# A scheduled attention-and-MLP kernel: two cross-engine latencies in the builder's simulation are changed, and the engine lists are made anew

## The chip, the cores and the metric

The kernel runs on one core of one Trainium2 chip. TensorE (PE) multiplies matrices, with its weight loads listed apart as PEld; VectorE (DVE), ScalarE (ACT) and GpSimd (POOL) do the elementwise work, and SyncE (SP) issues most of the DMAs. Each engine takes its own list of instructions in order and waits on semaphores that the others raise. The metric is the device time of one execution in microseconds (us).

## The reference

`x` has 2048 rows of 512. Part A goes through the sequence in 64 segments of 32 rows, and each segment needs eight memory rows that the segment before it made. Part B is an MLP over all rows. Cut to what matters:

```
for s in range(64):
    h = concat([mem, xs_s])                      # 8 memory rows and 32 rows of the sequence
    q, k, v = h @ Wq, h @ Wk, h @ Wv             # 32 heads of 128
    p = softmax(where(mask, q @ k.T * scale, -1e9))
    o = (p @ v) @ Wo
    mem = o[:8]; outs.append(o[8:])              # mem goes into the next segment
h  = x + concat(outs)                            # A works on layernorm(x)
h2 = h + gelu(layernorm(layernorm(h)) @ w1 + b1) @ w2 + b2
```

## The kernel before

The builder doesn't emit instructions as it goes. It records operations (`Op`: engine, tensors read and written, an assumed duration) into a `Sched` object, which then decides the order on every engine. TensorE's order is written out by hand (`ORDERS` and `EDGE`, for the segments in the middle and in the first and last block). For the other engines `schedule` ranks the operations by the longest path behind them (with a table of bonuses), then places them one by one, by rank, into the earliest stretch of their engine that is free in a simulation. The simulated start of an operation is the latest end of what it depends on plus `lat(p, o)`, a latency that depended only on the engine of the producer (`HOP`). The engine lists, and with them the semaphore waits, follow from the simulated starts. On the chip nothing of the simulated times is left, only the order.

Four segments of 32 rows make a block of 128 rows; I call them positions 0, 1, 2 and 3 of the block. One segment takes about 10.5 us and has on each half `r` of the heads this chain, with line numbers of the profile:

- TensorE makes K, Q and V of the segment (L676, and L417 where the weights stay loaded). ScalarE copies K and Q out of PSUM (`kq`, L690 and L691), and VectorE transposes them into `KALL` and `QX` (L713).
- TensorE makes the memory rows' scores (L831). `sc_softmax` follows: VectorE takes the maximum `nmc` (L839), ScalarE the exponentials `EC` (L843), VectorE the reciprocal `rsc` of their sum (L846), the product `PC` (L849) and its transpose `PTC` (L850).
- TensorE multiplies `PTC` with V (L861, L865), and the heads' output with Wo (L960). VectorE transposes that (`TT`, L972) and adds its halves into `hT` (L966), the memory rows of the next segment, with which TensorE starts over.

Work that can wait goes in between. `wo_B` puts the memory-row outputs of one whole block through Wo; VectorE transposes them into `TTB` (L985, position 3) and adds them into `opT` (L988, two instructions, position 0 of the next block). `nat` then turns a finished block: SyncE issues a DMA transpose of `opT` to `oN` (L993), VectorE adds it to the rows `xr` (L996) and takes their statistics (L999, L1000), GpSimd makes a scale of them (L1001, L1002), and SyncE writes the rows out (L1003). `ln1` prepares a block three ahead: statistics (L616, L617), scale on GpSimd (L618, L619), normalized rows `xn` (L620), a DMA transpose to `xT` (L637) and two GpSimd copies into `hT` and `hB` (L640, L639). The same SyncE list holds the transfers that spread a block's memory-row values over partitions, out to `v_last` (L773) and back into `VBD` (L778). GpSimd's copy into `QX` (L732) also belongs to every segment.

The two lines that the change speaks of by name are kinds of operations: `EC0` and `EC1` are the exponentials of the two halves, `hTm` is the sum that makes the memory rows (L966).

Of the kernel before, what the change touches and what calls it, by code (L numbers as in the profile page):

```python
# [16 lines left out]
ENGINES = ("pe", "act", "dve", "pool", "sp")  # L17
HOP = {"pe": 0.21, "act": 0.06, "dve": 0.05, "pool": 0.08, "sp": 2.0}
SWITCH = 0.12
OVERLAP = {"act": 0.1, "dve": 0.07, "pool": 0.05, "sp": 0.0}  # L20
DMA_SEMS, SOFT_SEMS = 100, 8
FETCH_N, FETCH_US, FETCH_OFF = 254.4, 3.5, 90
# [66 lines left out]
class Sched:  # L89
# [81 lines left out]
    @staticmethod  # L171
    def lat(p, o):
        if p.is_dma:
            return HOP["sp"]
        if p.eng == "pe" and o.eng == "pe":
            return 0.0
        return HOP[p.eng]

    def schedule(self):
        assert len(self.pe_order) == len(set(self.pe_order)) == sum(o.eng == "pe" for o in self.rec)  # L180
# [45 lines left out]
        for o in order:  # L226
# [5 lines left out]
            if o.eng == "pe":  # L232
                if o.prev is not None:
                    q = o.prev
                    t = max(t, q.start + q.dur + (SWITCH if q.mode != o.mode else 0.0))
                fetched += o.ni
# [7 lines left out]
            for eng, (fn, dur) in (o.alts or {o.eng: (o.fn, o.dur)}).items():  # L244
                L, ST = lines[eng], starts[eng]
                u = t
                while True:
                    i = bisect.bisect_right(ST, u)
                    while True:
# [3 lines left out]
                        if prev is not None:  # L253
                            s = max(s, prev.start + prev.dur - OVERLAP[eng])
                        if nxt is None or s + dur - OVERLAP[eng] <= nxt.start + 1e-9:
                            break
# [1057 lines left out]
```

## Time and profile before

| what | value |
|---|---|
| median of 3 runs | 830.18 us (829.86 to 830.25) |
| the profiled execution | 829.23 us, of which its span is 827.5 us |
| granted TensorE clock, mean | 0.994 |
| instructions | 46217 |
| DVE busy | 541.4 us (65%) |
| ACT busy | 581.2 us (70%) |
| POOL busy | 80.6 us (10%) |

A span runs from the first to the last instruction of the program. In a timeline a row has the start in us from the span's start, the busy time, engine, line, operation and operands, the count of instructions merged into it, and in brackets the idle time of the engine before it with what ended that. In the chain of work that ended last, a row has a start, a length and the work.

### The profile page before, as it was taken

To read this page: it belongs to the slowest core of one execution; us is meant where nothing else is said; L and a number is where in the kernel's file an instruction comes from. 1 tells how busy PE (TensorE), PEld (TensorE's weight loads), DVE (VectorE), ACT (ScalarE), POOL (GpSimd) and SP (SyncE) were. 2 spreads that over 40 slices of the span, in tenths; PEclk is the share of its full clock that TensorE was granted. 3 is DMA by queue.
4 is the path that set the end of the run, shared out by engine and by line. 5 is a ranking of instruction groups with operands and counts; after the bars stand their busy time and mean duration, and the time that the engine had idled before them with its cause. 6 is when DMAs were issued, how large, how long until landed. Compare 5 with 4: busy or idle time off the path is not lost.

```text
span 827.5 us, 46217 instructions
## 1 busy us (share of the span) xinstructions
PE 791.1 (96%) x22113; PEld 384.4 (46%) x19913; DVE 541.4 (65%) x1716; ACT 581.2 (70%) x1570; POOL 80.6 (10%) x210
## 2 busy tenths in 40 slices
PE   4788999999999999999999999999999998899998
PEld 1244444444545454545454545454545454554443
DVE  3258677777777777777777777777777777533211
ACT  2457787878787878787878787878787877533332
POOL 4002100001010001010100000000000000015200
PEclk9899999999999999999999999999999999999999
DMA  9960100111101111111110101000000111353310
GB/s 344 386 189 17 23 23 23 30 30 29 30 27 27 31 27 30 30 30 29 30 30 29 31 25 33 20 20 24 23 23 23 48 31 30 99 155 88 71 32 26
DMA packets 62283, 46.37 MB, mean 56 GB/s; under 512 B 28336, under 2 KB 58424, under 8 KB 62088
## 3 DMA queue, kind: packets, MB, share of 16 engines
q1 hardware_dynamic: 61692, 42.94, 17.5%
q8 instruction: 165, 2.70, 1.4%
q0 software_dynamic: 208, 0.33, 0.1%
q14 instruction: 30, 0.25, 0.1%
q10 hardware_dynamic: 188, 0.14, 0.1%
HBM read 28.98 MB, written 8.39 MB: 45 GB/s over the span
## 4 chain that ended last, share of the span: by engine, by line
PE 84%; ACT 5%; SPq 5%; DVE 4%; DMA 1%; issue 1%
PE ps L676 20%; PE ps L960 19%; PE quad L676 11%; PE quad L417 9%; PE ps L1196 6%; PE quad L1203 6%; PE ps L417 4%; PE quad L861 3%; ACT kq L690 3%; PE ps L831 3%; SPq L587 2%; SPq L602 2%; PE ps L889 2%; PE quad L918 1%; DVE KALL L713 1%; DMA WO<-in_A_Wo_dram 1%
## 5 line engine op out<-in xcount | busy, mean ns | idle before, releaser
L960 PE MATMUL ps<-WO,OT 128*32 128x256 bf16 x4224 | 140.7, 274 | 4.4 <-ACT OT L690 2.8
L676 PE MATMUL ps<-WV,hT 128*32 128x512 bf16 x1640 | 122.2, 381 | 0.0
L417 PE MATMUL quad<-WK,hT 128*32 128x512 bf16 x1204 | 112.1, 379 | 0.0
L960 PEld LDWEIGHTS ps<-WO,OT 128*32 128x32 bf16 x4224 | 94.9, 96 | 34.8 <-ACT OT L690 19.4
L972 DVE STREAM_TRANSPOSE TT<-ps 128x256 f32<-128x256 f32 x66 | 29.7, 450 | 107.5 <-PE ps L960 107.5
L690 ACT CAST OT<-quad 128x128 bf16<-128x128 f32 (+1 forms) x192 | 84.9, 442 | 20.7 <-PE quad L865 11.9
L690 ACT CAST kq<-quad 128x512 bf16<-128x512 f32 x128 | 69.5, 588 | 26.9 <-PE quad L417 23.9
L843 ACT ACTIVATE EC<-ps,nmc 128x64 f32<-128x64 f32 x256 | 78.0, 310 | 12.8 <-DVE nmc L839 4.9
L713 DVE STREAM_TRANSPOSE KALL<-kq 128x256 f32<-128x256 f32 x160 | 71.1, 445 | 22.1 <-ACT kq L690 17.2
L676 PE MATMUL quad<-WK,hT 128*32 128x512 bf16 x844 | 84.2, 389 | 0.0
L1199 ACT ACTIVATE WQ<-ps,b1t 128x512 bf16<-128x512 f32 x56 | 38.5, 687 | 58.7 <-PE ps L1196 58.7
L690 ACT CAST VS<-ps 128x512 bf16<-128x512 f32 x128 | 75.0, 586 | 2.5 <-PE ps L417 2.5
L676 PE MATMUL quad<-WQ,hT 128*32 128x512 bf16 x856 | 60.6, 380 | 5.2 <-DVE hT L966 5.2
L691 ACT ACTIVATE kq<-ps 128x512 bf16<-128x512 f32 x96 | 57.6, 600 | 8.4 <-PE ps L676 6.0
L676 PEld LDWEIGHTS quad<-WK,hT 128*32 128x32 bf16 x844 | 25.9, 99 | 80.3 <-issue 78.3
L901 ACT ACTIVATE SA<-SA 128x256 f32<-128x256 f32 x64 | 26.7, 417 | 51.5 <-DVE SA L900 50.6
L713 DVE STREAM_TRANSPOSE QX<-kq 128x256 f32<-128x256 f32 x128 | 56.3, 440 | 3.8 <-ACT kq L691 3.8
L676 PE MATMUL ps<-WQ,hT 128*32 128x512 bf16 x772 | 56.2, 379 | 0.0
L1203 PE MATMUL quad<-WK,WQ 128*128 128x512 bf16 (+1 forms) x228 | 54.6, 376 | 0.5 <-DVE WV L1255 0.5
L691 ACT ACTIVATE kq<-quad 128x512 bf16<-128x512 f32 x64 | 38.1, 595 | 19.3 <-PE quad L417 16.0
L843 ACT ACTIVATION_READ_ACCUMULATOR EC<-ps,nmc 128x1 f32 x256 | 50.4, 197 | 0.0
L1255 DVE TENSOR_TENSOR WV<-quad,WV 128x512 bf16<-128x512 f32 (+1 forms) x17 | 11.1, 659 | 56.7 <-PE quad L1203 50.0
(115 smaller groups left out, 1366.1 us busy)
## 6 DMA issues: line engine op xcount, KB each, us to landing
WV<-in_A_Wv_dram SPq DMA_DIRECT2D x4, 1024.0 KB, 9.7
WK<-in_A_Wk_dram SPq DMA_DIRECT2D x4, 1024.0 KB, 18.2
WQ<-in_A_Wq_dram SPq DMA_DIRECT2D x4, 1024.0 KB, 20.6
VBD<-v_last SPq DMA_DIRECT2D x63, 64.0 KB, 1.9
v_last<-hnT SPq DMA_DIRECT2D x60, 64.0 KB, 2.0
WO<-in_A_Wo_dram SPq DMA_DIRECT2D x3, 1024.0 KB, 20.0
h_mid<-xr SPq DMA_DIRECT2D x16, 128.0 KB, 2.3
WK<-in_B_w_dram SPq DMA_DIRECT2D x4, 512.0 KB, 3.9
```

The costliest lines, as they stand in the source:

```text
L417: return e.add_instruction(mybir.InstMatmult(name="I-%d" % (4000000 + _kept[0]), engine=mybir.EngineType.PE, start_tensor_calc=start, stop ...
L676: ins = e.matmul(o, l, m, start=(cc == ccs[0]), stop=(cc == ccs[-1]), tile_position=(0, 32 * j), skip_group_check=True)
L690: return {"act": (lambda e: e.copy(out, src), t_act(n, ps_)), "dve": (lambda e: e.tensor_copy(out, src), 0.16 + 1.042e-3 * n * fast)}
L691: return {"act": (lambda e: e.mul(out, src, scale_), t_act(n, ps_)), "dve": (lambda e: e.tensor_scalar(out, src, scale_, None, ALU.mult), ...
L713: S.op("dve", lambda e: e.transpose(out, src), reads=[("kq", i)], writes=[key], dur=t_dve(256) + 0.02)
L843: ins = e.activation(EC[:, r, sl, :], ps[bank][:, 64 * sl:64 * sl + 64], ACTF.Exp, bias=nmc[:, r, sl:sl + 1], accum_out=smc[:, r, sl:sl + 1])
L901: S.op("act", lambda e: e.activation(SA[:], SA[:], ACTF.Exp), reads=["SA"], writes=["SA"], dur=t_act(256, False))
L960: ins = e.matmul(ps[bank][32 * j:32 * j + 32, 0:256], lhs(slot(h)), wo_cols(h, b), start=(k == 0), stop=(k == 15), tile_position=(0, 32 * ...
L972: S.op("dve", lambda e: e.transpose(tt.rearrange("p c q t -> p (c q t)"), ps[bank][:, 0:256]), reads=[("ps", bank)], writes=[("TT", par)], ...
L1196: ins = e.matmul(ps[bank][:, 0:SBT], W1[:, cc, fc * P:(fc + 1) * P], hnT_of(k)[:, cc, :], start=(cc == 0), stop=(cc == DC - 1))
L1199: S.op("act", lambda e: e.activation(gT[:, fc, :], ps[bank][:, 0:SBT], ACTF.Gelu_apprx_tanh, bias=b1t[:, fc:fc + 1], scale=1.0), reads=[(" ...
L1203: S.op("pe", lambda e: e.matmul(quad[:, t, c], gT[:, fc, t * P:(t + 1) * P], W2[:, fc, c], start=(fc == 0), stop=(fc == FC - 1), skip_grou ...
```

## The change

A table `LAT` gives a latency to three kinds of producers, and `lat` looks there before it takes the engine's value. For the exponentials it is 0.18 in place of 0.06, for the memory rows' sum 0.15 in place of 0.05. No operation, duration or tile is changed.

```
+LAT = {"EC0": 0.18, "EC1": 0.18, "hTm": 0.15}
...
         if p.eng == "pe" and o.eng == "pe":
             return 0.0
-        return HOP[p.eng]
+        return LAT.get(p.kind, HOP[p.eng])
```

The table adds a line to the file, so that every line of the kernel after it has a number one higher: L988 before is L989 in the changed kernel. TensorE's and ScalarE's lists keep their order. VectorE's, SyncE's and GpSimd's don't. What moves is much the same in every block.

The first place is VectorE at position 0 of a block, around the softmax of the first half of the heads. Before:

```order
L713 STREAM_TRANSPOSE QX<-kq 128x8x32
L846 RECIPROCAL rsc<-smc 128x2
L839 TENSOR_REDUCE nmc<-ps 128x2
L849 TENSOR_TENSOR PC<-EC,rsc 128x2x64
L850 STREAM_TRANSPOSE PTC<-PC 128x64
```

And in the changed kernel:

```order
L714 STREAM_TRANSPOSE QX<-kq 128x8x32
L989 TENSOR_TENSOR opT<-TTB 64x16x8 x2
L847 RECIPROCAL rsc<-smc 128x2
L840 TENSOR_REDUCE nmc<-ps 128x2
L850 TENSOR_TENSOR PC<-EC,rsc 128x2x64
L851 STREAM_TRANSPOSE PTC<-PC 128x64
```

The two additions into `opT` now stand between the transpose of `QX` and the first reciprocal, in 13 blocks (segments 8, 12, ... 56).

The second place is the end of the same segment on VectorE, from the transpose of the second half's `PTC` to the sum that makes the memory rows. Before:

```order
L850 STREAM_TRANSPOSE PTC<-PC 128x64
L988 TENSOR_TENSOR opT<-TTB 64x16x8 x2
L972 STREAM_TRANSPOSE TT<-ps 128x256
L966 TENSOR_TENSOR hT<-TT 64x4x8 x2
```

And in the changed kernel:

```order
L851 STREAM_TRANSPOSE PTC<-PC 128x64
L997 TENSOR_TENSOR xr<-xr,oN 128x512
L1000 BN_STATS st<-xr 128x6
L973 STREAM_TRANSPOSE TT<-ps 128x256
L1001 BN_AGGR agg<-st 128x2
L967 TENSOR_TENSOR hT<-TT 64x4x8 x2
```

The place of the `opT` pair is taken by the sum with `oN` and the two statistics, which stood in position 1 before: L996 between `QX` and the first reciprocal, L999 and L1000 behind the second `PTC`. In their place at the end of position 1 now stand L616 and L617 (before at the end of position 2), and L620, which stood between `PTC` of the first half and the second reciprocal in position 3, stands there in position 2.

The third place is SyncE's list over one block. Before:

```order
L773 DMA v_last<-hnT 16x8x256 x4
L778 DMA VBD<-v_last 32x4x256 x2
L637 DMA_TRANSPOSE xT<-xn 128x4x128
L778 DMA VBD<-v_last 32x4x256 x2
L993 DMA_TRANSPOSE oN<-opT 128x4x128
```

And in the changed kernel:

```order
L774 DMA v_last<-hnT 16x8x256 x2
L638 DMA_TRANSPOSE xT<-xn 128x4x128
L774 DMA v_last<-hnT 16x8x256 x2
L779 DMA VBD<-v_last 32x4x256 x4
L994 DMA_TRANSPOSE oN<-opT 128x4x128
```

The transpose to `xT` now stands amid the transfers of position 2, one segment earlier, as L620 does, in nine blocks. On GpSimd the copy into `hB` stands directly behind the scale of `ln1`, and the larger copy into `hT` two copies into `QX` later; before, both stood together behind them.

In block 0, L620 of segments 2 and 3 moves ahead of the first reciprocal (in segment 3 with L617 behind that reciprocal), and one L620 leaves this place in segment 4. In the last block L966 into `opT` stands ahead of a second reciprocal in segment 60, and L996 in segment 61.

## The prediction

> **What bounds the kernel now.** I read the page first, its busy times and the chain that ended last.
>
> ```profile
> PE 791.1 (96%) x22113; PEld 384.4 (46%) x19913; DVE 541.4 (65%) x1716; ACT 581.2 (70%) x1570; POOL 80.6 (10%) x210
> PE 84%; ACT 5%; SPq 5%; DVE 4%; DMA 1%; issue 1%
> ```
>
> TensorE is busy for 96% of the span and makes 84% of the chain. Its order isn't touched, so the time can change only where TensorE waits for VectorE: by more waiting, or by less of the little that there is. The chain in order of time gives the pace, by the product with Wo that ends each segment:
>
> ```profile
> 218.26 1.43 PE ps L960 x48
> 228.75 1.44 PE ps L960 x47
> 239.38 1.43 PE ps L960 x48
> 250.10 2.09 PE ps L960 x70
> 260.72 1.44 PE ps L960 x48
> ```
>
> These are the ends of positions 0, 1, 2, 3 and 0 again. Positions 1, 2, 3 and 0 follow at 10.49, 10.63, 10.72 and 10.62 us. Positions 1 and 2 have the same matrix products; the 0.14 us between them is worth a look, since what VectorE does in position 2 is what the change makes it do in position 0.
>
> **The step that sets the price: a pair of additions ahead of the reciprocal.** VectorE's timeline in position 0, from the transpose of `QX` to the memory rows:
>
> ```profile
> 257.33 0.44 DVE L713 STREAM_TRANSPOSE QX<-kq 128x256 f32<-128x256 f32 x1
> 258.18 0.17 DVE L846 RECIPROCAL rsc<-smc 128x2 f32<-128x2 f32 x1 [0.41 <-ACT EC L843]
> 258.26 0.27 DVE L839 TENSOR_REDUCE nmc<-ps 128x2 f32<-128x128 f32 x1
> 258.78 0.24 DVE L850 STREAM_TRANSPOSE PTC<-PC 128x64 f32<-128x64 f32 x1
> 259.84 0.24 DVE L850 STREAM_TRANSPOSE PTC<-PC 128x64 f32<-128x64 f32 x1
> 260.12 0.59 DVE L988 TENSOR_TENSOR opT<-TTB 64x128 bf16<-64x128 f32 x2
> 262.21 0.45 DVE L972 STREAM_TRANSPOSE TT<-ps 128x256 f32<-128x256 f32 x1 [1.50 <-PE ps L960]
> 262.69 0.39 DVE L966 TENSOR_TENSOR hT<-TT 64x32 bf16<-64x32 f32 x2
> ```
>
> Before, the pair L988 (0.59 us) stands in the idle time ahead of `TT`, where it costs nothing: 1.50 us are still left. It moves into the 0.41 us in which VectorE waits for the exponentials. It is longer than that. How it sits there is shown by position 2, where a pair of the same kind, L966 into `opT`, already stands at this place:
>
> ```profile
> 235.89 0.44 DVE L713 STREAM_TRANSPOSE QX<-kq 128x256 f32<-128x256 f32 x1
> 236.36 0.52 DVE L966 TENSOR_TENSOR opT<-TT 64x96 bf16<-64x96 f32 x2
> 236.89 0.17 DVE L846 RECIPROCAL rsc<-smc 128x2 f32<-128x2 f32 x1
> 237.50 0.24 DVE L850 STREAM_TRANSPOSE PTC<-PC 128x64 f32<-128x64 f32 x1
> ```
>
> `QX` ends at 236.33, the pair starts 0.03 later, and the reciprocal 0.01 behind its end. With L988 in position 0 the reciprocal comes 0.03 + 0.59 + 0.01 = 0.63 us after the end of `QX` (257.77), at 258.40 in place of 258.18: **0.22 us late**. `PTC` of the first half is late by as much. Whether TensorE feels it is in its own rows, position 0 and then position 2:
>
> ```profile
> 258.81 0.39 PE L676 MATMUL ps<-WV,hT 128*32 128x512 bf16 x4
> 259.14 0.26 PE L861 MATMUL quad<-PTC,VS 32*128 32x16 bf16 x16
> 237.16 0.62 PE L676 MATMUL ps<-WV,hT 128*32 128x512 bf16 x8
> 237.80 0.26 PE L861 MATMUL quad<-PTC,VS 32*128 32x16 bf16 x16
> ```
>
> In position 2 `PTC` ends at 237.74 and L861 starts 0.06 later: TensorE waits for it. In position 0 it ends at 259.02 and L861 starts 0.12 later: 0.06 us to spare, no wait. So 0.22 - 0.06 = **0.16 us of waiting** each time. In blocks where VectorE's idle time is 0.38 in place of 0.41, the reciprocal is late by 0.03 more and the spare time is longer by as much; the difference stays. Thirteen blocks: 13 x 0.16 = **+2.1 us**. Position 2 checks it: its pair is 0.07 us shorter, so it should cost about 0.09, and the segment is 0.14 us longer than position 1. Nothing in the segment gives the time back: VectorE, ScalarE and the next `hT` all follow from TensorE.
>
> Queued behind the reciprocal are L839, ScalarE's second exponentials and the second `PTC`, 0.22 us late too. That one has room: before, it ends at 260.08 and its L861 starts at
>
> ```profile
> 260.41 0.27 PE L861 MATMUL quad<-PTC,VS 32*128 32x16 bf16 x16
> ```
>
> 0.33 later, where 0.06 is enough, and TensorE itself comes 0.16 later.
>
> **The end of position 0.** Here L996 waits for the DMA transpose of `opT`.
>
> ```profile
> 260.73 1.19 SPq L993 DMA_TRANSPOSE oN<-opT  x1
> DMA to landing us min/median/max: 2.3/2.3/4.8
> ```
>
> The first row is its issue, 0.02 us behind L988; the second, of that line alone, says that it lands 2.3 us after. With L988 ending at 258.39 it lands at 260.7; the second `PTC` ends at 260.30, so VectorE stands for some 0.4 us, then does L996 and L999 before `TT`:
>
> ```profile
> 225.72 0.38 DVE L996 TENSOR_TENSOR xr<-xr,oN 128x512 bf16<-128x512 bf16 x1
> 226.18 0.17 DVE L846 RECIPROCAL rsc<-smc 128x2 f32<-128x2 f32 x1
> 228.01 0.65 DVE L999 BATCH_NORM_STATS2 st<-xr 128x6 f32<-128x512 bf16 x1
> 228.69 0.18 DVE L1000 BATCH_NORM_AGGREGATE agg<-st 128x2 f32<-128x6 f32 x1
> ```
>
> 260.8 + 0.38 + 0.03 + 0.65 = 261.9, while `TT` can't start before 262.37. **Cost nothing**, with 0.5 us of cover; a transpose that lands later than that would delay the memory rows. L1000 then stands between `TT` and L966. Bounds: nothing, or all of its 0.18 + 0.03. The next instruction after such a small one starts early where it doesn't need it (L839 starts 0.08 after the reciprocal above), so I take 0.07. The memory rows have that much to spare:
>
> ```profile
> 263.29 0.84 PE L676 MATMUL quad<-WQ,hT 128*32 128x512 bf16 x12
> ```
>
> L966 ends at 263.08, the product starts 0.21 later, and 0.14 is the least seen (below). **Nothing** again, at worst 13 x 0.14 = 1.8 us.
>
> In position 1 the departure of L996 wins nothing: the reciprocal starts 0.08 us behind its end (226.10), not 0.01 as behind the pair in position 2, so the exponentials ended its wait and still will. L616 and L617 take the place of L999 and L1000, which are of the same kind, ahead of a `TT` that waits for TensorE. L620 goes from its place in position 3 to the same place in position 2; both hide it behind the second exponentials.
>
> **What the change may win: the block's end.** In position 3 the data of the `xT` transpose lands just when the memory rows are made, and GpSimd's copies slow VectorE:
>
> ```profile
> 251.86 0.51 POOL L640 COPY hT<-xT 128x384 bf16<-128x384 bf16 x1 [4.12 <-DMA xT<-xn]
> 252.07 0.58 DVE L966 TENSOR_TENSOR hT<-TT 64x32 bf16<-64x32 f32 x2
> 252.24 0.63 PE L960 MATMUL ps<-WO,OTB 128*32 128x256 bf16 x16
> 252.79 0.83 PE L676 MATMUL quad<-WQ,hT 128*32 128x512 bf16 x12
> 421.68 0.58 DVE L966 TENSOR_TENSOR hT<-TT 64x32 bf16<-64x32 f32 x2
> 294.69 0.63 PE L960 MATMUL ps<-WO,OTB 128*32 128x256 bf16 x16
> 295.13 1.05 PE L676 MATMUL quad<-WQ,hT 128*32 128x512 bf16 x16
> ```
>
> L966 takes 0.58 in place of 0.39, ends at 252.65, and TensorE starts 0.14 later, 0.55 after the row before it; where the copy misses L966 this is 0.44. That is 0.11 us, in three blocks (the last of them at 421.68), and some 0.07 in two others together: **-0.4 us** when it moves away. It moves to the same place in position 2, where only the shorter copy `hB` follows at once: between -0.4 and nothing, and I take -0.3. The long copy into `hT` then falls into position 3 beside the softmax.
>
> The trace shows which operations such a neighbour disturbs: L966 into `hT`, at 252.07. [...]
>
> ```profile
> L966 DVE TENSOR_TENSOR opT<-TT x128: 252/254/257, 73.7 to 732.1; 64x96 bf16<-64x96 f32 x128
> 247.44 0.29 POOL L732 COPY QX<-QTB 128x128 f32<-128x128 f32 x1 [3.53 <-PE ps L831]
> ```
>
> The 128 additions into `opT` took 252 to 257 ns, none longer, though this copy stands beside them in position 3.
>
> **Block 0 and the last block.** Segments 2 and 3 get L620 ahead of the reciprocal, and segment 3 also L617, a step like L1000: between nothing and 0.2 us each, once. In segments 60 and 61 the moved additions stand ahead of the second reciprocal, whose `PTC` has room, as above. I take +0.1 us in all.
>
> **Sum.** 2.1 + 0.1 - 0.3 = +1.9 us. The profiled execution took 829.23 us (span 827.5, 1.7 around it); it would take 831.1. The median lies 0.95 us above it, so the forecast is 830.18 + 1.9 = **832.1 us**.
>
> **Rivals.**
> - *The pair overlaps.* The reciprocal could start 0.08 us before the pair's end, as L839 does before the reciprocal's. Then 13 x 0.08 = 1.0, in sum +0.8 us, 831.0. Against it: 0.01 behind the pair in position 2. Chance 0.17.
> - *The block's end wins it back; not slower.* Position 3 is 0.09 us longer than position 2. If all of that belongs to the `xT` transpose, and position 2 bears it without loss, the nine blocks with a moved transpose give 0.8 us beside the 0.4: 2.2 - 1.2 = +1.0, 831.2, within what counts as the same; with L988 at half its price as above it is 830.1. It decides from the point where the relief of a block, over nine, outweighs the 0.16 us of L988 over thirteen: 0.23 us each. For it: the transpose leaves this segment. Against it: position 3 has other products (Wo for `wo_B`). Chance 0.13.
> - *A copy on GpSimd holds L988.* A wait of one copy, 0.29 us, makes 13 x 0.29 = 3.8 us more: 835.9. The row of 128 additions speaks against it. Chance 0.04.
> - *The transpose lands late, or L1000 costs all of its time.* 13 x 0.14 = 1.8 on top: 833.9. For it: VectorE now stands in its own list for a DMA. Against it: 0.5 us of cover. Chance 0.10.
>
> **How the numbers follow.** The forecast has 0.56. The range runs from 830.3 (the second rival's middle) to 834.1 (the fourth, and a little); outside remain the third and the far ends. A measurement tells 0.2% from no change, 1.7 us here: slower begins at 831.8. From the forecast's own spread of 0.8 us about two thirds lie above that (0.38), with the last two rivals 0.52. Faster takes more than any term allows: 0.05. Within: 0.43.
>
> **What would show it.** In the changed kernel's timeline at position 0: the pair between `QX` and the reciprocal, no idle time there, L861 0.06 behind `PTC`, and the segment at about 10.78 us. At its end idle time of VectorE put down to the DMA into `oN`, some 0.4 us, and still some ahead of `TT`. In position 3, L966 at 0.39 throughout. I am wrong if position 0 stays at 10.62, or if `TT` there starts without idle time before it.

## The result, and the profile after

| kernel | median | ratio to the kernel before, 95% interval |
|---|---|---|
| before | 830.21 us (4 runs) | |
| changed | 850.66 us (849.28 to 851.64, 4 runs) | 1.0246 [1.0227, 1.0264] |

The changed kernel is 20.5 us slower; 1.9 were forecast. The span of its profiled execution is 848.0 us at the same granted clock as before, 0.994. Its page, busy times and the chain that ended last:

```profile
PE 795.1 (94%) x22099; PEld 387.0 (46%) x19913; DVE 542.5 (64%) x1716; ACT 582.0 (69%) x1570; POOL 81.7 (10%) x210
PE 73%; DVE 8%; DMA 6%; ACT 6%; SPq 5%; issue 2%
```

The work is what it was. But TensorE makes 73% of the chain in place of 84%, and the DMA went from 1% to 6%. Position 0 on VectorE in the changed kernel, in the same block as shown before (start, length, engine, line, work, and in brackets the idle time before it):

```profile
261.52 0.45 DVE L714 STREAM_TRANSPOSE QX<-kq 128x256 f32<-128x256 f32 x1
262.00 0.59 DVE L989 TENSOR_TENSOR opT<-TTB 64x128 bf16<-64x128 f32 x2
262.62 0.17 DVE L847 RECIPROCAL rsc<-smc 128x2 f32<-128x2 f32 x1
...
264.28 0.24 DVE L851 STREAM_TRANSPOSE PTC<-PC 128x64 f32<-128x64 f32 x1
266.64 0.43 DVE L997 TENSOR_TENSOR xr<-xr,oN 128x512 bf16<-128x512 bf16 x1 [2.11 <-DMA oN<-opT]
267.10 0.69 DVE L1000 BATCH_NORM_STATS2 st<-xr 128x6 f32<-128x512 bf16 x1
267.71 0.43 DVE L973 STREAM_TRANSPOSE TT<-ps 128x256 f32<-128x256 f32 x1
268.07 0.14 DVE L1001 BATCH_NORM_AGGREGATE agg<-st 128x2 f32<-128x6 f32 x1
268.24 0.39 DVE L967 TENSOR_TENSOR hT<-TT 64x32 bf16<-64x32 f32 x2
```

VectorE stands 2.11 us for the DMA transpose (0.4 were foreseen), and there is no idle time left ahead of `TT`. TensorE in the same stretch:

```profile
263.00 0.39 PE L677 MATMUL ps<-WV,hT 128*32 128x512 bf16 x4
263.52 0.26 PE L862 MATMUL quad<-PTC,VS 32*128 32x16 bf16 x16
...
265.04 1.50 PE L961 MATMUL ps<-WO,OT 128*32 128x256 bf16 x48
...
267.45 0.41 PE L677 MATMUL ps<-WV,hB 128*32 128x512 bf16 x4
268.77 0.83 PE L677 MATMUL quad<-WQ,hT 128*32 128x512 bf16 x12 [0.91 <-DVE hT L967]
```

Two waits are to be seen. L862 starts 0.52 us after the row before it, where it was 0.33: 0.19 more, the price of L989 (forecast 0.16). And the next segment starts late: its data, L961's product, ended at 266.54, and `TT` took it at 267.71. The transpose into `oN`, by its own line (who waited for it, in us and times, and its landing):

```profile
  DVE xr L997: 27.9, 14
...
DMA to landing us min/median/max: 2.3/4.0/4.6
```

Before, it was 2.3/2.3/4.8. A third loss stands in position 3 of the last six of the 13 blocks (segments 39, 43, ... 59), and is no wait for another engine:

```profile
462.82 0.42 PE L890 MATMUL ps<-KALL,QX 128*24 128x32 bf16 x32
463.12 0.38 PE L677 MATMUL quad<-WQ,hT 128*32 128x512 bf16 x1
463.98 0.83 PE L677 MATMUL quad<-WQ,hT 128*32 128x512 bf16 x11 [0.49 <-issue]
```

"issue" means that the profile shows nothing that TensorE waited for; one matmul of the product runs, and the next comes 0.86 us later. I call this a starved start.

The length of a position is the time from one `TT` to the next. The one ahead of this position 0 stands in VectorE's timeline at

```profile
255.90 0.45 DVE L973 STREAM_TRANSPOSE TT<-ps 128x256 f32<-128x256 f32 x1 [2.10 <-PE ps L961]
```

so that it takes 267.71 - 255.90 = 11.81 us, where it was 10.62. Summed over the 13 blocks (segments 8 to 59), from the starts of `TT` in each trace:

| kernel | median us | position 0 | 1 | 2 | 3 |
|---|---|---|---|---|---|
| before | 830.2 | 137.0 | 136.4 | 138.2 | 139.6 |
| changed | 850.7 | 152.9 | 136.6 | 138.1 | 144.2 |
| nat_back | 832.6 | 139.1 | 137.1 | 138.2 | 139.4 |
| xn_back | 847.0 | 155.6 | 136.2 | 138.2 | 139.4 |
| after_pad4 | 847.2 | 153.3 | 136.2 | 138.2 | 139.8 |
| after_pad | 831.6 | 139.8 | 136.5 | 138.5 | 139.2 |
| after_pad101 | 839.3 | 140.5 | 140.1 | 140.2 | 139.3 |
| after_pad33 | 854.4 | 158.2 | 138.5 | 138.2 | 139.8 |
| before_pad | 842.0 | 145.4 | 138.5 | 139.0 | 140.8 |
| before_pad75 | 830.8 | 139.4 | 136.4 | 138.3 | 139.2 |
| opt_late | 826.8 | 136.6 | 136.4 | 136.8 | 138.5 |
| opt_late75 | 828.1 | 138.8 | 136.4 | 137.2 | 137.4 |

Position 0 holds 15.9 us of the loss, position 3 holds 4.6. Of the 15.9, L989 takes 13 x 0.19 = 2.5; the late transpose takes the other 13.4.

**What makes the transpose late.** The DMA view of one window gives packets and MB by queue. From the issue to the landing, before:

```profile
q1 hardware_dynamic: 544, 0.13, 25.2%
issues: line engine op xcount, KB each, median us to landing
oN<-opT SPq DMA_TRANSPOSE x1, 2.3
```

And in the changed kernel:

```profile
q1 hardware_dynamic: 544, 0.13, 14.6%
q8 instruction: 1, 0.02, 1.6%
issues: line engine op xcount, KB each, median us to landing
oN<-opT SPq DMA_TRANSPOSE x1, 4.0
```

The transpose has its 544 packets in both. In the changed kernel one packet of another kind falls among them: q8 brings TensorE's instructions, 16 KB at a time (165 packets, 2.70 MB, in the changed kernel); I call such a packet a fetch or a refill. Before, that packet had gone ahead of the issue; in the window from 259.9 to 260.73, the issue:

```profile
q8 instruction: 1, 0.02, 6.6%
```

In the changed kernel 542 of the 544 packets have started by 2.1 us after the issue at 262.61, as all of them have before. The fetch runs from 264.48 to 265.48, and the last two packets, of 4 bytes each, start as it ends. The window from 265.4 to 266.61, the landing, holds nothing else:

```profile
q1 hardware_dynamic: 2, 0.00, 0.1%
```

So the end of the transpose waits for the fetch. In the twelve traces of this study (segments 8 to 59) there are 89 transposes with packets left over when a fetch ends more than 2.1 us after the issue; in all 89 the next of these packets starts within 0.03 us of that end.

Counting TensorE's instructions in the trace against the starts of q8's packets shows when the fetches come. A packet serves 256 instructions (165 packets for 42278 of them in the changed kernel), and a block of four segments has 2560 of them before the change, so the refills fall on the same places of every block. In the kernel before, a fetch starts some 0.65 us ahead of the `oN` issue. The change moves that issue 2.3 us forward in the segment, and in 11 of 13 blocks the transpose is late; where the trace holds both, the next fetch starts 1.9 to 2.6 us after the issue, with the transpose under way. In the two others (issues at 350.11 and 392.95) it comes at 2.33 and 2.34, all 544 packets have gone by then, and the transpose lands after 2.3 and 2.4; position 0 takes 10.7 us there and 11.7 to 12.4 in the rest.

### The profile page after: what moved, and what is told of

Its sections match the earlier page's. It is cut to its first block, busy times and chain, and to the rows that moved or that the text cites. A ratio compares the mean times of both kernels' runs of the same rounds, so it can differ in the third digit from the quotient of the medians.

```text
span 848.0 us, 46194 instructions
## 1 busy us (share of the span) xinstructions
PE 795.1 (94%) x22099; PEld 387.0 (46%) x19913; DVE 542.5 (64%) x1716; ACT 582.0 (69%) x1570; POOL 81.7 (10%) x210
## 4 chain that ended last, share of the span: by engine, by line
PE 73%; DVE 8%; DMA 6%; ACT 6%; SPq 5%; issue 2%
PE ps L961 16%; PE ps L677 15%; PE quad L677 11%; PE quad L418 9%; PE ps L1197 6%; PE quad L1204 6%; DMA oN<-opT 5%; ACT kq L691 4%; PE ps L418 3%; PE quad L862 3%; SPq L588 2%; PE ps L832 2%; SPq L603 2%; DVE KALL L714 1%; PE ps L890 1%
## 5 line engine op out<-in xcount | busy, mean ns | idle before, releaser
L961 PE MATMUL ps<-WO,OT 128*32 128x256 bf16 x4224 | 140.5, 274 | 3.9 <-ACT OT L691 2.8
L418 PE MATMUL quad<-WK,hT 128*32 128x512 bf16 x1204 | 115.0, 379 | 0.0
L961 PEld LDWEIGHTS ps<-WO,OT 128*32 128x32 bf16 x4224 | 95.1, 96 | 34.0 <-ACT OT L691 19.4
L677 PE MATMUL quad<-WK,hT 128*32 128x512 bf16 x844 | 86.9, 389 | 0.0
L677 PE MATMUL quad<-WQ,hT 128*32 128x512 bf16 x856 | 63.1, 380 | 18.9 <-DVE hT L967 16.7
L677 PEld LDWEIGHTS quad<-WK,hT 128*32 128x32 bf16 x844 | 27.6, 99 | 78.5 <-issue 73.6
L677 PEld LDWEIGHTS ps<-WQ,hT 128*32 128x32 bf16 x772 | 23.8, 97 | 52.6 <-issue 40.7
```

The lines of the kernel that those rows point to most:

```text
L418: return e.add_instruction(mybir.InstMatmult(name="I-%d" % (4000000 + _kept[0]), engine=mybir.EngineType.PE, start_tensor_calc=start, stop ...
L677: ins = e.matmul(o, l, m, start=(cc == ccs[0]), stop=(cc == ccs[-1]), tile_position=(0, 32 * j), skip_group_check=True)
L961: ins = e.matmul(ps[bank][32 * j:32 * j + 32, 0:256], lhs(slot(h)), wo_cols(h, b), start=(k == 0), stop=(k == 15), tile_position=(0, 32 * ...
```

## The experiments

Theory F: the fetch in the flight makes the transpose late. Rival G: the place of the issue does it, by SyncE's list or its neighbours on VectorE and GpSimd. A few small matmuls at TensorE's start shift all refills against the program and leave the order on every engine.

**after_pad**: the changed kernel, 75 small matmuls (150 instructions) at its start, whose result nothing reads. The simulation sees no time in them, so the lists stay.

```
-PAD = 0
+PAD = 75
...
-            S.op("pe", f, reads=["ident"], writes=[("ps", bank)], dur=0.05 * n, mode=MC, ni=2 * n)
+            S.op("pe", f, reads=["ident"], writes=[("ps", bank)], dur=0.0, mode=MC, ni=0)
```

> The changed kernel with 75 small matmuls (150 TensorE instructions) ahead of the first K product, at the program's start; every engine's order is otherwise that of the changed kernel. Theory F (instruction fetches): the DMA transpose of opT lands late because one of TensorE's 16 KB instruction fetches starts 1.9 us after its issue, inside its flight; the fetches come every 4.2 us, ten to a block, at a place fixed by the count of TensorE's instructions. 150 instructions more move them by 2.5 us to an earlier place, 0.6 us ahead of the issue, where they stood in the kernel before. Then L994 lands 2.3 us after its issue in all blocks, VectorE waits for oN about 0.4 us in place of 2 us, the starved starts of position 3 vanish too, and the time is 831.5 to 834 us (830.2 and 13 x 0.19 of L988). Rival G (the place in SyncE's and VectorE's lists makes the transpose late, whatever is fetched): the order is unchanged, so the time stays at 850 to 852 us and L994 lands after 4.0 to 4.6 us.

831.63 us (10 runs), ratio 1.0022 [1.0012, 1.0031]. Nothing but 150 idle instructions was added, and 19 us are gone. VectorE in position 0:

```profile
262.32 0.43 DVE L997 TENSOR_TENSOR xr<-xr,oN 128x512 bf16<-128x512 bf16 x1 [0.45 <-DMA oN<-opT]
262.78 0.69 DVE L1000 BATCH_NORM_STATS2 st<-xr 128x6 f32<-128x512 bf16 x1
263.92 0.45 DVE L973 STREAM_TRANSPOSE TT<-ps 128x256 f32<-128x256 f32 x1 [0.45 <-PE ps L961]
```

This is the picture that the prediction drew: 0.45 us of standing for the transpose (0.4 foreseen), then L997 and L1000, then 0.45 us of cover ahead of `TT` (0.5 foreseen). F holds, G falls: the order on VectorE, ScalarE, GpSimd and SyncE in this trace is that of the changed kernel.

**before_pad**: the kernel before with 33 such matmuls (66 instructions), by the same edit.

> The kernel before with 33 such matmuls (66 TensorE instructions) at the same place; all orders are otherwise those before. Theory F: the fetches move 1.1 us to an earlier place, so those that started 2.7 to 3.9 us after the issue of the two DMA transposes now start 1.6 to 2.8 us after it. L993 then lands after about 4 us, which costs nothing since L996 comes 5 us later; L637 lands after 3.5 us or more, and the late fetch starves TensorE at the start of position 0 in some of nine blocks, as it did at the start of position 3 in the changed kernel (0.5 to 0.9 us each): 831 to 837 us. Rival G: 830.2 us, L993 lands after 2.3 us.

842.01 us (4 runs), ratio 1.0147 [1.0128, 1.0166]: the direction was right, the size not. The landing goes to 2.3/4.0/4.5 and nobody waits for it in these blocks; what costs is TensorE itself at the start of position 0, here its weight loads:

```profile
257.35 0.21 PEld L676 LDWEIGHTS quad<-WQ,hT 128*32 128x32 bf16 x6
258.13 0.33 PEld L676 LDWEIGHTS quad<-WQ,hT 128*32 128x32 bf16 x10 [0.57 <-issue]
```

It stops after a few instructions, in all 13 blocks, and position 0 is 0.46 to 1.0 us longer for it. To say where it stops I number TensorE's instructions from the first one in the trace and start anew after each 256; that number is the index below. The stops have one place, the index 191 or 192, in nearly all that were seen in this study. Here the start of position 0 has the index 177, so TensorE, which takes the first products of a segment fast (in the kernel before 16 weight loads in 0.58 us from 252.76, then four each 0.43 us), reaches the index 192 before the refill is there. In the kernel before, the index there is 114 to 117, and 192 comes later in the segment.

**nat_back**: the changed kernel with L996's sum held behind `QX` of position 1, where it stood before; L989 stays early, and L620 falls back to position 3.

```
-            xs = xr[:, bk % XR, :]
+            if whole:
+                nat_sum(bk)
+
+        def nat_sum(bk, after=()):
...
+                    if n == "Q1" and sg == 1 and bk > 1:
+                        nat_sum(bk - 2, [S.last_writer["QX", s % 2, 1]])
```

> The changed kernel with L996 held behind the transpose of QX of position 1, as before. With it L999, L1000, L616, L617, L620 and SyncE's list fall back to the places before: what is left of the change is the early opT pair (13 blocks) and block 0. Theory F: the transpose of opT still lands late (about 4 us), but nobody waits for it; the time is that of the early pair alone, 13 x 0.19 = 2.4 us: 832 to 833.5 us. Rival: the late transposes cost something by themselves (they hold up the instruction fetch, and TensorE starves somewhere): 835 us or more. Rival of the prediction, that the pair costs less than 0.1 us each: below 831.5 us.

832.62 us (7 runs), ratio 1.0028 [1.0017, 1.004]. TensorE, and the landing:

```profile
259.86 0.39 PE L677 MATMUL ps<-WV,hT 128*32 128x512 bf16 x4
260.37 0.26 PE L862 MATMUL quad<-PTC,VS 32*128 32x16 bf16 x16
```

```profile
  DVE xr L1000: 1.5, 1
...
DMA to landing us min/median/max: 2.3/4.2/4.6
```

The transpose is as late as in the changed kernel, but only one execution of the sum (L1000 in this file) ever waits for it. So the late transposes, of 4.2 us in the median, cost next to nothing here, where VectorE doesn't stand for them, and what is left is L989: 0.51 us from row to row, where it was 0.52 in the changed kernel and 0.33 before.

**xn_back**: the changed kernel with L620 of blocks 7 to 15 held behind the first `PTC` of position 3, so that the `xT` transposes are back at their old place.

```
-                 reads=[("xr", tb % XR), ("ag", i), ("rs", i)], writes=[("xn", i)], dur=0.38)
+                 reads=[("xr", tb % XR), ("ag", i), ("rs", i)], writes=[("xn", i)], after=[ptc.get(4 * (tb - 5) + 3)], dur=0.38)
...
+                    if n == "SC0" and sg == 3 and bk > 1:
+                        ptc[s] = S.last_writer["PTC", 0]
```

> The changed kernel with L620 of blocks 7 to 15 held behind the first PTC of position 3; SyncE's list is then that of the kernel before, and the early opT pair and L996, L999, L1000 at the end of position 0 stay as changed. Theory F: the waits for oN stay (about 13 us of the loss), the starved starts of position 3 vanish (about 4 us): 845 to 848 us. Rival: the early transpose to xT is what makes the transpose of opT late (they share SyncE's queue): then both vanish, 832 to 834 us.

847.00 us (4 runs), ratio 1.0201 [1.0184, 1.0218]. The starved starts of position 3 are gone, the late `oN` transposes stay, now in all 13 blocks, which makes position 0 longer by another 2.7 us. I had put the starved starts down to the `xT` transposes' own traffic. But four of the six blocks with such a start have no `xT` transpose any more. The count shows another reason: with the `xT` transposes at their new place, TensorE has one wait instruction fewer in each of nine blocks, 2559 in place of 2560. The index at the start of position 3 goes from 195 down to 186, and from 188 on TensorE stops there: 192 now lies just behind the start, not just ahead of it. The fetch comes later too, 1.6 to 2.1 us ahead of the start there in place of 3.0.

**after_pad4**: the changed kernel with 4 small matmuls, to tell the two apart.

> The changed kernel with 4 small matmuls (8 instructions) at TensorE's start. The trace of the changed kernel has one wait instruction of TensorE fewer in each of the nine blocks with a moved xT transpose, so that the refill boundary drifts: at the start of position 3 the instruction index in its 256 goes from 195 to 186, past 192, where TensorE needs the next refill; in xn_back, where L620 is back, it stays at 195. Theory D (the starved starts of position 3 come from this drift): 8 instructions put the index at 203 to 194, TensorE is not starved there in any block, position 0 keeps its late oN transposes: 845.5 to 848.5, as xn_back. Rival X (the starved starts come from the moved xT transposes, which hold up TensorE's fetch): nothing changes, 849 to 852, with starved starts in six blocks.

847.18 us (5 runs), ratio 1.0205 [1.0185, 1.0225]. The index now goes from 204 to 195, no start of position 3 is starved, and position 0 is as in the changed kernel:

```profile
267.56 0.42 DVE L997 TENSOR_TENSOR xr<-xr,oN 128x512 bf16<-128x512 bf16 x1 [2.04 <-DMA oN<-opT]
```

Eight instructions at the start are worth 3.5 us. The theory of the drift holds, that of the traffic falls.

**before_pad75**: the kernel before with the pad of after_pad, for a comparison of both at one place of the refills.

> The kernel before, with the same 75 small matmuls at TensorE's start as after_pad. A block takes exactly 2560 TensorE instructions, ten fetches of 256, so a pad shifts the refills against all blocks alike: with 150 instructions the refill boundary stands near 0.02 at the start of position 0, as in after_pad, instead of 0.45. Theory (the time depends on where the refills fall): fetches start about 1 us after the oN issue, which lands late (+3 to +4) with nobody waiting, and no refill falls due in the fast start of a segment: 829.5 to 831.5. Then after_pad stands above it by the price of L989 alone, 1.5 to 3 us, less what the pad itself costs both (0.5 to 1). Rival (any shift of the kernel before costs some 12 us, as the first pad did; its place was the lucky one): 838 to 844.

830.84 us (10 runs), ratio 1.0012 [0.9997, 1.0027], as expected. after_pad stands 0.8 us above it, not 1.5 to 3: position 0 of before_pad75 is 2.4 us longer than before, since 192 falls into its start. In eight of the 13 blocks TensorE's weight loads go on 0.1 to 0.5 us late there, in three of them 0.4 to 0.5, and the median of position 0 goes from 10.51 to 10.75. So at this place of the refills the change costs 0.8 us, which the two intervals don't tell from nothing, and its own price and the refills' don't simply add.

**after_pad101** and **after_pad33**: the changed kernel with two more places of the refills.

> The changed kernel with 101 small matmuls (202 instructions) at TensorE's start: the refill boundary stands near 0.23 at the start of position 0 instead of 0.44, so the fetch that started 1.9 to 2.2 us after the oN issue should start some 0.9 us later, near +2.9, when the transpose has landed. Theory (only a fetch within about 2.3 us after the issue delays the transpose): L994 lands +2.3 again, position 0 takes 10.6 to 10.8 us: 831 to 835, with a few short waits for instructions wherever 0.75 then falls. Rival (a fetch before the issue, as in after_pad, is needed to keep the two apart; or any neighbour within 4 us delays it): L994 still lands +4, 845 to 852.

839.31 us (4 runs), ratio 1.0119 [1.01, 1.0138]. The landing is 2.3/2.4/5.1 as the theory said, position 0 short again. But only the first two blocks test it: there the fetch starts 3.07 and 2.52 us after the issue, and the transpose lands after 2.3 and 2.4, which speaks against the rival. In the other eleven the fetch has gone ahead of the issue by 0.3 to 0.8 us, as in after_pad. The size was missed, since 192 now falls into fast stretches of positions 1 and 2. One of them, in the weight loads:

```profile
481.34 0.38 PEld L677 LDWEIGHTS quad<-WQ,hT 128*32 128x32 bf16 x12
482.82 0.31 PEld L677 LDWEIGHTS quad<-WK,hT 128*32 128x32 bf16 x4 [1.10 <-issue]
```

> The changed kernel with 33 small matmuls (66 instructions): the boundary near 0.69, as in before_pad; the fetch starts near +0.9 after the oN issue, still inside the flight, and TensorE reaches the end of what it holds 15 instructions into the fast start of position 0. Theory (both effects stand beside each other): L994 lands at +3.0 to +4.0, and TensorE stands for instructions at the start of position 0, 0.4 to 1 us in each block, as in before_pad: 842 to 856. Rival (a fetch in the first 1.2 us of the flight, before the transpose's data move, delays nothing; the starved start of position 0 alone remains): L994 +2.3, 840 to 844.

854.37 us (4 runs), ratio 1.0296 [1.0258, 1.0335]: both effects stand in one block, as the first theory said. TensorE's weight loads at the start of position 0, and VectorE at its end:

```profile
260.97 0.22 PEld L677 LDWEIGHTS quad<-WQ,hT 128*32 128x32 bf16 x7
262.31 0.33 PEld L677 LDWEIGHTS quad<-WQ,hT 128*32 128x32 bf16 x9 [1.12 <-issue]
```

```profile
270.52 0.43 DVE L997 TENSOR_TENSOR xr<-xr,oN 128x512 bf16<-128x512 bf16 x1 [0.90 <-DMA oN<-opT]
```

In the first five blocks, where the fetch starts 0.35 to 0.39 us after the issue, the transpose lands after 2.8 to 3.0. In the others, where it starts 1.3 to 2.0 after, it lands after 3.6 to 5.0.

**opt_late**: the kernel before with the lesson of L989 used the other way. In positions 2 and 3 it has a pair ahead of the first reciprocal too (L966 into `opT`); it is held behind the second `PTC`.

```
+            if xrows and 0 < s < NS - 1 and s % 4 in (1, 2):
+                held.append(s)
+            elif xrows:
+                wo_rows(s)
...
+                    if n == "SC1" and held:
+                        wo_rows(held.pop(), [S.last_writer["PTC", 1]])
```

> The kernel before, with the L966 additions into opT of positions 2 and 3 held behind the second PTC, so that no pair stands ahead of the first reciprocal. Theory (a pair ahead of the reciprocal costs what it makes the reciprocal late): the TensorE step into L861 falls from 0.41 to 0.31 in two segments of 13 blocks, 2.6 us: 827.2 to 828.2. Rival (VectorE only shifts the wait, as the additions then stand ahead of TT): 829.8 to 831. Third: the shorter segments shift SyncE's transposes into a fetch of TensorE: 832 or more.

826.82 us (5 runs), ratio 0.9954 [0.994, 0.9968]: faster than both kernels, and 0.4 us below what the theory expected. VectorE in position 2:

```profile
236.06 0.43 DVE L713 STREAM_TRANSPOSE QX<-kq 128x256 f32<-128x256 f32 x1
236.91 0.17 DVE L846 RECIPROCAL rsc<-smc 128x2 f32<-128x2 f32 x1 [0.41 <-ACT EC L843]
...
238.57 0.24 DVE L850 STREAM_TRANSPOSE PTC<-PC 128x64 f32<-128x64 f32 x1
238.85 0.52 DVE L966 TENSOR_TENSOR opT<-TT 64x96 bf16<-64x96 f32 x2
...
240.93 0.45 DVE L972 STREAM_TRANSPOSE TT<-ps 128x256 f32<-128x256 f32 x1 [0.64 <-PE ps L960]
```

The reciprocal waits for the exponentials again, and 0.64 us are still free ahead of `TT`. TensorE's step into L861 falls from 0.43 and 0.42 to 0.33 and 0.32 us (medians of positions 2 and 3), and the two positions are 1.3 and 1.0 us shorter over the 13 blocks.

**opt_late75**: the same with the pad of 75.

> opt_late with the 75 matmuls at the start. Theory: as far below before_pad75 as opt_late is below the kernel before, 2 to 3 us, if the refills stay harmless in both: 827.5 to 829. Rival (the place of the refills decides more than the additions): the two pads differ by more than 3 us in one direction.

828.08 us (6 runs), ratio 0.9969 [0.9958, 0.9981]: 2.8 below before_pad75, as expected. The gain stands at both places of the refills.

## Why the prediction was wrong, point by point

- **The pair ahead of the reciprocal** (+2.1): right. 0.19 us a block were measured for 0.16, and nat_back, where it is alone, took 0.28% more than the kernel before, 2.3 us. L989 took its 0.59 us beside GpSimd's copies, so the rival of a copy that holds it is out. But in each of the 13 blocks its second addition started first, 0.11 us ahead of the copy. The 0.29 us of this rival, a wait of one copy, was an estimate that no run shows: where a copy started first, as once in block 1 of the changed kernel (the second addition of L967 into `opT`, at 84.23), the addition takes 0.47 us for 0.25, 0.22 more; so its price stays open for another place in the list. The reciprocal starts 0.03 us behind the pair's end, so the rival of a pair that overlaps it is out too.
- **The end of position 0** ("Cost nothing, with 0.5 us of cover; a transpose that lands later than that would delay the memory rows"): this step failed. Its arithmetic is right, as after_pad shows to 0.05 us. Its input was wrong: I took 2.3 us from issue to landing as a property of the transpose. It was one of this place, 0.65 us behind a fetch of TensorE's. The 4.8 in the same row said that it can be otherwise, and I didn't ask when. At the new place it is 4.0, since the last packets wait for a fetch, and 13.4 of the 20.5 us come from it; moving the fetch, in after_pad, takes 13.1 us off position 0. The rival "the transpose lands late" named the wait but priced L1000 alone, 1.8 us; its own condition, a landing more than 0.5 us late, was exceeded by 1.1 to 1.8 us in 11 blocks.
- **L1000 between `TT` and L966** (nothing): right as long as `TT` isn't late. In after_pad, where it isn't, position 0 takes 10.69 us in eight of the 13 blocks for 10.51, which is the price of L989 alone. In the changed kernel TensorE waits for `hT` anyway and starts 0.14 us behind it, the least seen before.
- **The block's end** (-0.3): too small to be told from the rest in the medians. In the table it belongs to position 0, since L966 into `hT` comes behind `TT`: in the kernel before, five blocks with a slowed L966 ahead of them take 10.53 to 10.63 us there and the other eight 10.50 or 10.51, 0.4 us in all. In after_pad no L967 into `hT` is slowed in these blocks.
- **What TensorE waits for** ("the time can change only where TensorE waits for VectorE"): this premise failed too. In the changed kernel position 3 is 4.6 us longer, by a path that the prediction doesn't have. TensorE's list was taken to be unchanged, and its order is; the waits in it are not. One instruction fewer in each of nine blocks moved the refills past the start of position 3, and there TensorE waits for its own instructions.
- **Position 1 and block 0**: right as far as the traces show. Position 1 has 136.6 us for 136.4. In block 0 segments 1 to 3 take 30.76 us for 30.62, where 0.1 was forecast.

## What to carry to other kernels

A transfer's time from issue to landing, read in one place, holds for that place (here 2.3 us at the old one and 4.0 at the new); before its wait is moved into an engine's list ahead of work on the critical path, look at the longest landing in the row and at what else was on the DMA engines then, instruction fetches too. Where TensorE runs one unrolled list, busy for 94 to 96% of the span as here, a few instructions more or fewer at its start can be worth more than the edit that is being measured (8 of them 3.5 us and 150 of them 19, where L989 costs 2.5): compare at two pads before an order is judged. A wait that is 0.4 us long is no place for 0.6 us of work, even of work that has to be done somewhere: it cost 0.19 us a block.

## What the runs showed of the hardware

- TensorE's instructions come in packets of 16 KB on their own DMA queue (165 of them, 2.70 MB, in the changed kernel's page). Its trace has 42278 TensorE instructions, waits included, which makes 256 to a packet.
- A packet took 0.9 to 1.4 us in nine cases of ten in segments 8 to 59 of the twelve traces, and 2.7 at most. Where TensorE stopped for want of one, it stopped at the index 191 or 192 in nearly all cases that were counted, and went on 2.2 to 3.1 us after the packet's start.
- The 128 x 512 DMA transpose of `opT`, left alone, landed 2.3 to 2.4 us after its issue. A fetch that started 1.2 to 2.1 us after the issue delayed that to 3.6 to 5.0 us, one that started 0.8 to 1.2 us after it (before_pad75, opt_late75) to 3.4 to 4.2, and one at 0.4 us to 2.8 to 3.0. Between 2.2 and 2.6 us both were seen: of eleven such fetches six delayed it, to 4.2 to 4.6, and five didn't. From 2.7 us on, or ahead of the issue, none did. In one block of after_pad and of after_pad101 the transpose landed after 2.9 with the fetch ahead of the issue; a packet of another instruction queue, q14, starts there 1.7 us after it.
- Where the fetch ended more than 2.1 us after the issue, the delay was a wait for that end (in all of the 89 transposes counted above). Between the last packets of a transpose that was held so and its landing 0.6 to 1.2 us pass in which the trace shows none of its packets (0.3 in the one left alone at 260.73); what happens in them stays open.
